# A hand-ordered attention and MoE kernel: both halves of V of pair 2 issued by ScalarE, of pair 3 by GpSimd, w_in issued further up, and the first quarter's loads and compute in another order

## The chip, the cores and the metric

The kernel runs on one core of one Trainium2 chip. The metric is the device time of one execution in microseconds (us). Before the change three runs took 309.12, 309.83 and 308.51 us, median 309.12. Five engines run their own instruction queues side by side: TensorE (PE), VectorE (DVE), ScalarE (ACT), GpSimd (POOL) and SyncE (SP), which here only issues transfers. ACT and POOL issue transfers too: those of SP and ACT go to hardware queues, those of POOL to a software queue. An engine works its queue strictly in order, so an instruction that waits holds up all that stand behind it on that engine.

## The reference

Attention over 8 batches, 8 heads, 576 tokens of 64 numbers, followed by a two-layer network over all 4608 tokens.

```python
q_d, k_d, v_d = means of q, k, v over groups of 4 tokens
out_d = softmax(scale * q_d @ k_d.T) @ v_d          # 144 x 144 per head
out_up = np.repeat(out_d, 4, axis=2)
mask = np.abs(pos[:, None] - pos[None, :]) < 4
scores = np.where(mask, scale * q @ k.T, -1e9)      # 576 x 576 per head, a band
attn_out = out_up + softmax(scores) @ v
x = attn_out as (4608, 512)
h = x @ w_in                                        # 512 x 2048
g = h - np.tanh(h)
result = g @ w_out                                  # 2048 x 512
```

## The kernel before

**Tiling.** Heads are worked in 32 pairs p (two heads side by side on the partitions), four pairs to a batch. Of the band only blocks around the diagonal are computed. Each batch of 576 tokens then goes through the network as one block: 512 of its tokens in 16 chunks of the hidden width, the remaining 64 of several batches together.

**What one pair does.** Its q and k (`st`, 256 KB each; for pairs 4 to 7 the buffers are named `Tw`) are cast to bf16 into `qr` (L550), transposed on PE (L557) and copied out of PSUM as `kt` (L562) and `kq` (L567). The last 64 tokens of all four pairs of a batch come as `sr`, are cast to `rr` (L540) and transposed and copied as `rT` (L580, L584), and each pair takes its part of them (L612, L617; "the rests"). Sums over four tokens are made on PE for the first pairs (L664, L667) and copied out as `qkd` (L672), and for later ones by adding on POOL or DVE through `half` (L649, L653, L643). Scores follow in two groups: the band (L701) and then the last band block with the pooled part (L711, L717); three exponentials on ACT write them to `E` (L722, L726, L730). The band part is multiplied by the mask (L757). V comes in two halves, one per head, as `vst` (160 KB each), is cast to `vw` (L476) and pooled by PE into `vp` (L507, L511). The product with V is L771; a reciprocal and a product on DVE (L787, L789) normalise it to `ln`, PE transposes that back (L814), and DVE joins the two parts into `xT` (L820, L807).

**The network.** For batch 0 the hidden layer takes a chunk of w_in and one column block of `xT` per matmul (L848), which lets it begin when the first pairs of the batch are ready; ACT takes the tanh (L860) and DVE subtracts (L863). w_in and w_out are loaded by POOL in four pieces each (L457, L461).

**What sets the order.** Every operation is recorded with what it reads and writes. `TURNS` is a table of numbers, two digits each, that lists all operations in the order in which they are emitted; it thereby sets the order on each engine. `ENGINES` gives, where an operation may run on more than one engine, a letter for the one that takes it (A, D or P). `BANKS` gives the PSUM bank of each tile, `FILL` puts dummy matmuls in front of some PE operations (17 ahead of the first, one at seven other places; L1524), and `BEHIND` adds waits that keep DVE and POOL in a chosen order at their common port to SBUF. Nothing is planned at run time. Transfers of the hardware queues take their completion semaphores in turn from a set of eight, counted over SP and ACT together: a new transfer waits until the eighth one before it has landed.

**The places that the change touches.** `load_v` (L407) issues the two halves of V of a pair; `ASIDE` (L301) lists the halves that ACT issues in place of SP: half 0 of pair 2 and half 0 of pair 3. Those two stand in ACT's queue behind the rests of pair 0 and 1 and ahead of `qkd` of pair 1. `load_w` issues the weights. The table's head up to about its 18th row, the first two rows of `ENGINES` and `BANKS`, and `FILL` and `BEHIND` hold what concerns the first batches.

Of the kernel before, what the change touches and what calls it, by code (L numbers as in the profile page):

```python
# [101 lines left out]
def kernel(  # L102
# [9 lines left out]
    nc = tc.nc  # L112
    B, H, S, D = q.shape
# [10 lines left out]
    STEP = 112  # L124
# [30 lines left out]
        "000I0J0G0H0307060E0F0K0L04050Q0R010O0P0W0X0e0f0C0M0N0S0T100Y0Z110g0h020a0b1215130D0A160U"  # L155
        "0V171H1P18141I0B1J191L1Q1A1K1R221M1N0m0n0i0j1O242R231T1j1k1B251S1C1f1d1g1e1u1U0c0d1W1v1w"
        "2S1y0k0l1x2Z091V2I2J0y2T082G2H1z1D2V291E2W0o0p261F2U1X1l1m212X27201n1o2z1Y2b1Z0z391p1q2a"
        "0q0r2d282c2n2o1r1G2e311h1i1s2f2p2q2g2A2K2L322Y1t3A3B2B2O2y5H2C3C3D302D2P3G5I332E1a353E0s"
        "0t2M2N5J34362v2h2F373N3O5K5L5P2i1b5e5f383F0u0v5M5S2w5N2r2s2j5O5Q3H5U5R3I3J5v662Q2k683K5B"
        "5T1c635E5V3L3d2l5C5x2m643j3k5y3M3l3e5D5F3f3g5X3p3q5W0w0x3m3h3v3r3n3w3i3P3Q5w3s5Y3t2t2u3o"  # L160
        "413x615k5l3y3u5z3z4243604744404D4E4548623T3U495Z654A464F4G4B4J6b5a674H4P3V3W4Q6B4R2x4K4L"
        "4I696c4S5g5h4M6e4C4N3X3Y3R3S5s5b6g6A4V4W4b4O6d4c5c4d4T4X5d4Y6U4h5t4U4i4Z5m5n4j4e4k6T4a6C"
        "4l4n6V6D4o6E4f4t4u4p6W4v4g6X6Z6f6F6Y7A6j4z4q6G5G4w4m504r513Z3a526H6a5556534s577B6Q4x5854"
        "7f7C6R7g4y6h3b3c7D597E72887F6i8d8e5A5u7I6k7G71896l7l6m74758E8F7H8j736n6y76778k6z966o7J6K"
        "6L977K6I6J9C7L5i5j7m8K6p5q5r7M6w6x8L7N7r7O5o5p8p78CF6M6N9D79CC7s6u6v7x9f8Q6q6r7y9g6s6t8R"
        "9Z9I9a8S8q9T9b9cCG7z9h9i7X9jCE6O6P7Y7b9k7P7Q7Z9J9l9v9w7c6SCB8v9t9u7d8w9U7V7WCD9O8x9P7R7S"
        "7eAA9m9W7h9V9X9Y7i7a7n9QCH7o7j9nAB7p7k7t70ACAD809d9o9p849eAGAd7uA1A27qAe9q9zA0AH7vA79r81"
        "7T7U9sA8BD857w82ELEMAIAh9x9y86838AAgAJ8B878GAiAjCI8H8C8MAEAM8VAFATAU8I8NAVAW8DAm8WAKAbAc"
        "Ao8J8O8ZB0B18XAL8aBGBH8fAq8PAn8gAN8Y8bBFB2B38l8h8cA9ApAk8m8iBEAt8rAOBMBIBJ8sAP8n8yAr8z8o"
        "8tDt92BcBdBN908u93AXAYBAAl91DyIgIh989EBaBbAs9FBBENEO94CJBOBPBgBh99BQ9K95Dx9AAuBiDzE09G9L"  # L170
        "9BBqEaBKBrBLE39HA5A6CLCMEJEKAv9MBsAwE4B8B9BtBRBkBlByBTEb9NE5A3A4BjE6E7BzEcEdBSCREACSCKAQ"
# [37 lines left out]
        "APADDADAADPPDDPPDDADDDDAPPDADDAADDDPDDDDDAADDADAADDDAAADDDPPAPPPAADAPPPDAAPAPADADPPPDDAA"  # L209
        "APADAAPPPDAAPPDDAAPPPDDAAAADDPDADDAADDDDAPPPDDPPDAAAPPAAPPDDAAPPPAAPPDDPPADDADDADAAPPDAP"  # L210
# [7 lines left out]
        "0123453012067016731120212706021330112130022310312010302101013121001113020110023303011200"  # L218
        "2131010210231012301102321001203101010110123031002311201210012130120131010102030210302321"
# [4 lines left out]
        "15717 2b71 2A71 3B41 2D11 5S31 3H31 6671"  # L224
    )
    BEHIND = (
        "0211 1H12 1D1V 0z20 1t2f 5I30 5Q5N 635B 5w5W 6562 6c2x 6d6A 5u6i AACD ABCH AmAF AnAL DxC"
        "J F8CZ FfFD DFFn MUFt GAGb IrJ6 JNK7 MZJs NBKu OELA LqNn ODLO O7OQ QoNy RYOp RZP8 T3Rd S"
        "WPQ PiSi TVTU TaRk TPUO TnUY TmTO WZU7 WeWc WfVu XWX6 XcXP Z5Yy ZqZ4 ZpZH"
# [71 lines left out]
    ASIDE = ((2, 0), (3, 0))  # L301
# [105 lines left out]
    def load_v(p):  # L407
        b, j, s = p // NP, p % NP, seat_v(p)
        for i in range(2):
            base = v[b, 2 * j + i]  # L410

            aside = (p, i) in ASIDE

            def issue(i=i, base=base, aside=aside):
                (nc.scalar if aside else nc.sync).dma_start(out=vst[s][:, i], in_=bass.AP(
                    tensor=base.tensor, offset=base.offset,
                    ap=[[D, 128], [STEP * D, NT], [1, D]]))
# [1138 lines left out]
```

## Time and profile before

| | |
|---|---|
| median of three runs | 309.12 us |
| profiled execution, its own time | 309.13 us |
| its span in the profile | 307.4 us |
| mean granted PE clock | 0.992 |
| PE busy | 296.4 us, 96% |
| DVE, ACT, POOL busy | 266.6, 224.1, 157.2 us |

The span runs from the first instruction to the last; 1.73 us of the profiled time lie around it. PE's time is given as busy time with the idle time ahead of an instruction put down to what ended it; a stretch of PE at the half clock counts as busy. In a line such as `L717 <- ACT qkd L672` the first line is what waited and the second what released it; tiles are shown without their buffer numbers, so `E` is that of either parity of pairs. A row of the timeline gives start and duration in us, and a row that ends in `q` after the engine's name (ACTq, SPq) is the issuing of a transfer.

### The profile page before, as it was taken

What the parts mean: (1) busy time and instruction counts of PE and PEld (TensorE: products, weight loads), DVE (VectorE), ACT (ScalarE), POOL (GpSimd) and SP (SyncE); (2) the same over time, 40 slices, a digit from 0 to 9 for tenths busy, and PEclk for the clock granted to TensorE, in tenths of its full rate; (3) what the DMA queues carried; (4) which work ended last, traced back from release to release, by engine and by line L of the source; (5) the groups of instructions that cost most, each with busy time, mean ns of one, the idle gap of its engine ahead of it and who ended that gap; (6) DMA issues with size and microseconds to landing.
All of it is one profiled execution on the core that took longest, in us unless ns stands there. A gap on an engine that the chain in (4) does not pass through costs nothing.

```text
span 307.4 us, 8109 instructions
## 1 busy us (share of the span) xinstructions
PE 296.4 (96%) x3091; PEld 210.9 (69%) x3100; DVE 266.6 (87%) x493; ACT 224.1 (73%) x403; POOL 157.2 (51%) x213
## 2 busy tenths in 40 slices
PE   8598999999999999999999999999999999999994
PEld 3476555545577755875577755555988888889983
DVE  2578888679998988999998889999999999998783
ACT  2588786279888786988958988898877898875300
POOL 5247756026864466337873278456524364626550
PEclk9979999999999999999999999999999999999999
DMA  7999999999999999999899999979989426000333
GB/s 220 271 264 249 246 228 152 210 235 220 218 241 281 242 216 234 291 175 273 210 262 220 284 222 173 278 193 260 188 227 218 146 28 189 1 3 2 136 122 87
DMA packets 121191, 60.83 MB, mean 198 GB/s; under 512 B 88896, under 2 KB 119104, under 8 KB 121152
## 3 DMA queue, kind: packets, MB, share of 16 engines
q1 hardware_dynamic: 114656, 54.94, 76.5%
q0 software_dynamic: 4224, 4.19, 8.3%
q10 hardware_dynamic: 2272, 1.18, 1.6%
q8 instruction: 24, 0.39, 0.5%
q14 instruction: 15, 0.12, 0.1%
HBM read 44.04 MB, written 9.44 MB: 174 GB/s over the span
## 4 chain that ended last, share of the span: by engine, by line
PE 88%; DVE 5%; DMA 4%; issue 1%; ACT 1%; ACTq 0%; SPq 0%; DVEq 0%
PE ps L1284 27%; PE ps L848 26%; PE ps L958 8%; PE ps L771 6%; PE ps L996 5%; PE ps L1142 4%; PE ps L701 3%; PE ps L1114 2%; PE ps L1081 2%; DMA st<-in_q_dram 2%; DMA sr<-in_q_dram 2%; PE ps L814 1%; DVE E L757 1%; PE ps L717 1%; PE ps L507 1%
## 5 line engine op out<-in xcount | busy, mean ns | idle before, releaser
L848 PE MATMUL ps<-xT,w_in_sb 128*128 128x512 bf16 x384 | 91.5, 379 | 0.0
L1284 PEld LDWEIGHTS <-gT 128*128 128x128 bf16 x672 | 64.5, 98 | 12.3
L863 DVE TENSOR_TENSOR gT<-ps,u 128x512 bf16<-128x512 f32 x96 | 64.2, 684 | 6.8 <-ACT u L860 5.6
L860 ACT ACTIVATE u<-ps 128x512 f32<-128x512 f32 x96 | 56.4, 599 | 16.3 <-PE ps L848 14.5
L848 PEld LDWEIGHTS <-w_in_sb 128*128 128x128 bf16 x384 | 35.4, 98 | 35.6
L550 POOL CAST qr<-st 128x512 bf16<-128x512 f32 x42 | 25.4, 613 | 41.3 <-DVE Tw L1193 15.5
L1284 PE MATMUL ps<-w_out_sb,gT 128*128 128x256 bf16 x336 | 43.4, 273 | 0.0
L1284 PE MATMUL ps<-Tw,gT 128*128 128x256 bf16 x336 | 42.5, 273 | 0.0
L722 ACT ACTIVATE E<-ps 128x912 bf16<-128x912 f32 x32 | 29.9, 934 | 7.1 <-PE ps L711 5.8
L789 DVE TENSOR_TENSOR ln<-ps,r 128x768 bf16<-128x768 f32 x32 | 30.6, 955 | 0.8
L628 ACT COPY kt<-kq 128x576 bf16<-128x576 bf16 x23 | 27.3, 1185 | 1.4 <-DMA kq<-qr 1.1
L757 DVE TENSOR_TENSOR E<-E,mask 128x1152 bf16<-128x1152 bf16 x31 | 23.5, 760 | 3.8 <-ACT E L726 3.5
L771 PEld LDWEIGHTS <-E 128*128 128x128 bf16 x576 | 21.9, 98 | 6.0 <-DVE E L757 1.4
L638 POOL TENSOR_TENSOR half<-kq 128x576 f32<-128x576 bf16 x16 | 20.5, 1279 | 8.4 <-ACT u L860 3.5
L730 ACT ACTIVATE E<-ps 128x576 bf16<-128x576 f32 x32 | 21.0, 657 | 1.4 <-PE ps L717 1.4
L771 PE MATMUL ps<-vw,E 128*128 128x65 bf16 x320 | 19.2, 195 | 1.3 <-DVE E L757 1.0
L643 POOL TENSOR_TENSOR qkd<-half 128x288 bf16<-128x288 f32 x21 | 16.7, 797 | 5.8 <-DVE r L787 2.0
L1219 DVE TENSOR_TENSOR gT<-gT 128x2048 bf16<-128x2048 bf16 x14 | 17.2, 1231 | 0.2
L1370 POOL TENSOR_TENSOR y<-y,keep 128x512 f32<-128x512 f32 x8 | 10.2, 1278 | 13.4 <-DVE E L757 4.8
L996 PE MATMUL ps<-xT,w_in_sb 128*128 128x128 bf16 x256 | 16.8, 219 | 0.0
L1306 ACT COPY y<-ps 128x512 f32<-128x512 f32 x19 | 11.0, 587 | 7.5 <-PE ps L1284 6.7
L771 PE MATMUL ps<-vpr,E 128*128 128x65 bf16 x128 | 16.5, 195 | 0.0
(183 smaller groups left out, 596.4 us busy)
## 6 DMA issues: line engine op xcount, KB each, us to landing
vst<-in_v_dram SPq DMA_DIRECT2D x54, 160.0 KB, 4.2
st<-in_q_dram SPq DMA_DIRECT2D x28, 256.0 KB, 3.7
st<-in_k_dram SPq DMA_DIRECT2D x28, 256.0 KB, 5.0
out_dram<-y SPq DMA_DIRECT2D x14, 512.0 KB, 4.3
v<-in_v_dram SPq DMA_DIRECT2D x20, 256.0 KB, 2.7
w_in_sb<-in_moe_w_in_dram POOLq DMA_DIRECT2D x4, 512.0 KB, 8.4
w_out_sb<-in_moe_w_out_dram POOLq DMA_DIRECT2D x4, 512.0 KB, 6.6
vr<-in_v_dram SPq DMA_DIRECT2D x8, 128.0 KB
```

What stands on the lines that cost most here:

```text
L550: (eng, ns, lambda dst=dst, src=src, fn=fn: fn(out=dst, in_=src), port)
L628: ("ACT", 1180, lambda: A.copy(out=ktv, in_=src), False),
L722: A.activation(out=E[s][:, :, E0:E0 + 456], in_=at(s1)[:, :, PS0:512], func=AF.Exp, scale=SCALE)
L757: eng.tensor_tensor(out=el, in0=el, in1=mask.unsqueeze(1).to_broadcast([128, 2, S]), op=ALU.mult)
L771: T.matmul(po[:, hh, 65 * n:65 * n + 65], E[s][:, hh, e:e + 128], vv, start=start, stop=stop)
L789: op("DVE", 960, lambda: V.tensor_tensor(out=ln[s].rearrange("p n (h d) -> p h n d", d=D), in0=blocks()[:, :, :, 0:64], in1=r[s].unsqueeze ...
L848: T.matmul(at(name)[:, 0, :], w_in_sb[:, dc, fc * 128:(fc + 1) * 128], xT[dc][:, c0:c0 + S].rearrange("p (c g) -> p c g", c=4)[:, :, 0:128 ...
L860: op("ACT", 600, lambda: A.activation(out=u[us], in_=at(name)[:, 0, :], func=AF.Tanh), reads=[("hd", kb, fc)], writes=[("u", us)], uses=[n ...
L863: op("DVE", 690, lambda: V.tensor_tensor(out=gT[g][:, fc, :], in0=at(name)[:, 0, :], in1=u[us], op=ALU.subtract), reads=[("hd", kb, fc), ( ...
L958: T.matmul(at(("hz", kb, G, bk))[:, 0, 256 * x:256 * x + 256], left(k, x), right(k), start=(first and x == 0 and k == 0), stop=(k == 1), s ...
L996: T.matmul(at(name)[:, 0, 128 * f:128 * f + 128], w_in_sb[:, dc, (f0 + f) * 128:(f0 + f) * 128 + 128], xT[dc].rearrange("p (b c g) -> p b ...
L1284: T.matmul(dst, left[:, f, 128 * j:128 * j + 128], right[:, f, :], start=(first and e == 0 and f == 0 and (j == 0 or apart)), stop=(e == 1 ...
```

## The change

`ASIDE` becomes a table `WAY` with the engine that issues each half of V: both halves of pair 2 go to ACT, both of pair 3 to POOL, all others stay on SP. The heads of `TURNS`, `ENGINES` and `BANKS` are others, and with them the order of the loads and of the compute of the first two batches. One line is added, so line numbers above 412 are higher by one.

```diff
-    ASIDE = ((2, 0), (3, 0))
+    WAY = {(2, 0): "ACT", (2, 1): "ACT", (3, 0): "POOL", (3, 1): "POOL"}
...
-            aside = (p, i) in ASIDE
-
-            def issue(i=i, base=base, aside=aside):
-                (nc.scalar if aside else nc.sync).dma_start(out=vst[s][:, i], in_=bass.AP(
-                    tensor=base.tensor, offset=base.offset,
-                    ap=[[D, 128], [STEP * D, NT], [1, D]]))
-            load(680 if aside else 500, issue, [("vst", s, i)], 940, 10 * p - 3000 + 5,
-                 eng="ACT" if aside else "SP")
+            eng = WAY.get((p, i), "SP")
+
+            def issue(i=i, base=base, eng=eng):
+                {"SP": nc.sync, "ACT": A, "POOL": GP}[eng].dma_start(
+                    out=vst[s][:, i], in_=bass.AP(
+                        tensor=base.tensor, offset=base.offset,
+                        ap=[[D, 128], [STEP * D, NT], [1, D]]))
+            load({"SP": 500, "ACT": 680, "POOL": 770}[eng], issue, [("vst", s, i)], 940,
+                 10 * p - 3000 + 5, eng=eng)
...
     FILL = (
-        "15717 2b71 2A71 3B41 2D11 5S31 3H31 6671"
+        "15717 2b71 2A71 3B41 2D11 5S31 3H01 6601"
     )
     BEHIND = (
-        "0211 1H12 1D1V 0z20 1t2f 5I30 5Q5N 635B 5w5W 6562 6c2x 6d6A 5u6i AACD ABCH AmAF AnAL DxC"
+        "0211 1H12 1u1A 2S1V 280y 2y3F 5C5W 5G6A 737H 9fCB 9UCE AhAg AnAF A9AL DyAs DxCJ F8CZ FfF"
```

Eighteen rows of `TURNS` and two each of `ENGINES` and `BANKS` differ. From the work on the left-over tokens of the first batches on, at about 84 us of the trace before, PE's order is the same in both; so is that of the other engines from about there on.

ACT's queue from its two transfers on, before (`vst2` and `vst3` are V of pairs 2 and 3, `E0` and `E1` the scores of even and odd pairs, `L726` the last band block, `L730` the pooled part):

```order
L415 DMA vst3_86<-in_v_dram 128x5x64
L415 DMA vst2_85<-in_v_dram 128x5x64
L672 CAST qkd1_100<-ps_138 128x2x144
L722 ACTIVATE E0_113<-ps_138 128x2x456
L726 ACTIVATE E0_113<-ps_138 128x2x120
L730 ACTIVATE E0_113<-ps_138 128x2x2x144
L562 COPY kt0_96<-ps_138 128x512
L476 CAST vw0_88<-vst0_83 128x10x64
L730 ACTIVATE E1_114<-ps_138 128x2x2x144
L722 ACTIVATE E1_114<-ps_138 128x2x456
```

And ACT's queue in the changed kernel, from a cast of q of pair 1 that POOL did before:

```order
L551 CAST qr1_93<-st1_74 128x2x4x64
L613 COPY kt0_96<-rT0_81 128x4x16
L415 DMA vst2_85<-in_v_dram 128x5x64 x2
L673 CAST qkd1_100<-ps_138 128x2x144
L723 ACTIVATE E0_113<-ps_138 128x2x456
L731 ACTIVATE E0_113<-ps_138 128x2x2x144
L727 ACTIVATE E0_113<-ps_138 128x2x120
L723 ACTIVATE E1_114<-ps_138 128x2x456
L551 CAST qr0_92<-st2_75 128x2x4x64
L731 ACTIVATE E1_114<-ps_138 128x2x2x144
L727 ACTIVATE E1_114<-ps_138 128x2x120
```

Both transfers are now V of pair 2, at the same place ahead of `qkd1`. Behind them ACT has the copy of `kt` and the cast of V of pair 0 no longer this early, and in their place, ahead of the odd pair's last exponentials, a cast to `qr0`: q of pair 2, which DVE did before as soon as it had landed.

POOL's queue behind the constants, before (`qr1` from `st1` is pair 1; `vrp` and `vpr0` are V sums of the last tokens):

```order
L550 CAST qr1_93<-st1_74 128x2x4x64 x2
L442 TENSOR_TENSOR vrp_107<-vrs_106 128x64
L550 CAST qr0_92<-st2_75 128x2x4x64
L445 TENSOR_TENSOR vpr0_111<-vrp_107,hsel_108 128x520
L476 CAST vw1_89<-vst1_84 128x10x64
L457 DMA w_in_sb_71<-in_moe_w_in_dram 128x4x512
L476 CAST vw3_91<-vst3_86 128x10x64
L550 CAST qr1_93<-Tw1_135 128x2x4x64 x2
L457 DMA w_in_sb_71<-in_moe_w_in_dram 128x4x512
L649 TENSOR_TENSOR half_98<-kt0_96 128x144x2
```

And in the changed kernel (`st3` is q of pair 3):

```order
L551 CAST qr1_93<-st1_74 128x2x4x64
L551 CAST qr0_92<-st2_75 128x2x4x64
L415 DMA vst3_86<-in_v_dram 128x5x64 x2
L551 CAST qr1_93<-st3_76 128x2x4x64
L458 DMA w_in_sb_71<-in_moe_w_in_dram 128x4x512
L758 TENSOR_TENSOR E1_114<-E1_114,mask_66 128x2x576
L477 CAST vw3_91<-vst3_86 128x10x64
L458 DMA w_in_sb_71<-in_moe_w_in_dram 128x4x512
L551 CAST qr0_92<-Tw0_134 128x2x4x64
L477 CAST vw2_90<-vst2_85 128x10x64
L541 CAST rr1_80<-sr1_78 128x2x4x64
L458 DMA w_in_sb_71<-in_moe_w_in_dram 128x4x512
```

The two halves of V of pair 3 are issued by POOL behind the cast of k of pair 2. The first piece of w_in stands directly behind the cast of q of pair 3, where it stood behind the cast of V of pair 1; the multiplication of `E1` by the mask, DVE's before, stands behind it on POOL, and the casts of V of pair 2 and of `rr1` are POOL's too.

On PE the sums of pair 1 (L664) stand ahead of the scores of pair 0, the pooled scores of pair 0 ahead of all scores of pair 1, and the transposes of q of pair 2 behind those of k of pair 3 and the pooled scores of pair 1. The sums of pairs 2 and 3 stand ahead of the pooling of V of pair 0 and the output of pair 0. Four groups that stood ahead of the first L848, namely the transposes of k and q of pair 5, the first scores of pairs 4 and 5, the back transposes of pairs 2 and 3, and the pooled scores and V pooling of pair 4, now stand between the first L848s or behind them. On SP the two second halves of V of pairs 2 and 3 are gone, the second half of pair 1 stands one place further up ahead of k of pair 4, V of pair 4 stands ahead of q and k of pair 5, and about five later loads stand ahead of the two first transposing transfers.

More of the change, by code (lines that the diff above doesn't have):

```diff
@@ L154 @@
     TURNS = (
[L155 to L169, printed above, removed]
@@ new lines @@
+        "1E1F0p5e0d0z2a1X2b2c2g1Y281Z2d1r1s1t1a1k0s1b1c1m302z1G2A2B3B3C2C2e2f3D2v2w2O2P3E3F2D3G2h"
+        "2i31353H322N362y0u2j333437380r3d2E2F5Q5I5P3I5R2k3j3k5S3e5U3J1q2l2m3K3L3p3q3v3w3M3f3g3r3s"
+        "2o3x3h2Q3t2H5H5T5X3i0t5E7T5F3l3m3y0w5V1i5B3u5J5L3n3z5K41422L5M5k4344404748492s3R5g4A3o4D"
+        "5O645N63655v3VAX4B4C4E4F3Q454J4K4L4G6s3T4M5w4666670v4P4V5W4Q4W4X4Y4N4H4I685h4O5C5D0x2u4Z"
+        "4a4R4S4T4U6B4b4c2x3X694d4h4i4j4e4f4g5x5y4n4o6q6U6t4k4l4p4q4r4t4u5z6T4m5Y5Z4z555f6050625m"
```

26 lines of the change are left out of this document (18 added, 8 removed).

## The prediction

> **What bounds the kernel now.** The page first:
>
> ```profile
> span 307.4 us, 8109 instructions
> PE 296.4 (96%) x3091; PEld 210.9 (69%) x3100; DVE 266.6 (87%) x493; ACT 224.1 (73%) x403; POOL 157.2 (51%) x213
> PE   8598999999999999999999999999999999999994
> ```
>
> PE is busy for 96% of the span, and the change takes no matmul away. What can be won or lost is PE's idle time, and the third row puts it at the start and in the last slice. The view by stretches of time says how much (columns: stretch; busy us of PE, its weight loads, DVE, ACT and POOL; granted PE clock; DMA share and rate):
>
> ```profile
> 10.00:15.00 5.00, 2.35 (x46) 1.83 (x41) 2.35 (x9) 1.85 (x4) 0.87 (x2) 1.00 1.18 266
> 15.00:20.00 5.00, 4.42 (x60) 3.71 (x59) 3.29 (x10) 4.21 (x10) 2.33 (x3) 0.66 1.20 272
> 20.00:25.00 5.00, 4.71 (x85) 3.66 (x84) 4.49 (x10) 4.80 (x11) 2.40 (x5) 1.00 1.16 234
> 25.00:30.00 5.00, 3.77 (x78) 2.92 (x77) 4.14 (x11) 4.40 (x10) 3.87 (x6) 1.00 1.20 264
> 30.00:35.00 5.00, 5.00 (x55) 2.97 (x54) 4.14 (x13) 3.49 (x8) 4.71 (x7) 1.00 1.21 213
> ```
>
> Idle time is 2.65, 0.58, 0.29 and 1.23 us in the first four rows, 4.75 together, and nothing from 30 us on. The orders of the two kernels meet again at about 84 us, so the tail is the same work. **The most that this change can win is therefore 4.75 us, and what the half clock of the second row costs; the most that it can lose has no such bound.** PE's waits from 7 to 31 us by cause (total, times, longest):
>
> ```profile
> PE ps L717 <- ACT qkd L672: 2.3, 1, 2.3
> PE ps L771 <- DVE E L757: 0.8, 1, 0.8
> PE ps L814 <- DVE ln L789: 0.4, 1, 0.4
> PE ps L771 <- DVE vp L511: 0.4, 1, 0.4
> PE ps L557 <- ACT E L722: 0.4, 1, 0.4
> PE ps L557 <- POOL qr L550: 0.3, 2, 0.2
> PE ps L664 <- ACT E L730: 0.2, 1, 0.2
> ```
>
> These sum to 4.8: the list is complete. The largest wait is followed back in the chain of waits (start, us, what) and in ACT's timeline:
>
> ```profile
> 6.86 5.86 DMA st<-in_q_dram
> 11.17 1.95 ACTq L415 DMA_DIRECT2D vst<-in_v_dram  x2
> 13.15 0.40 ACT L672 CAST qkd<-ps 128x288 bf16<-128x288 f32 x1 [3.82 <-DMA st<-in_q_dram]
> 13.45 0.94 ACT L722 ACTIVATE E<-ps 128x912 bf16<-128x912 f32 x1
> 14.27 0.38 ACT L726 ACTIVATE E<-ps 128x240 bf16<-128x240 f32 x1
> 14.52 0.67 ACT L730 ACTIVATE E<-ps 128x576 bf16<-128x576 f32 x1
> 15.05 0.62 ACT L562 COPY kt<-ps 128x512 bf16<-128x512 bf16 x1
> 17.95 0.68 ACT L550 CAST qr<-Tw 128x512 bf16<-128x512 f32 x1
> 25.89 0.31 ACT L617 COPY kq<-rT 128x64 bf16<-128x64 bf16 x1
> ```
>
> ACT has nothing to compute for 3.82 us, because its two V issues occupy its queue for 1.95 us, from 11.17 to 13.12. The second can't be issued before a load of q has landed at 12.72 (6.86 + 5.86), whose completion semaphore it takes over; only then comes qkd of pair 1, and PE, which needs it, stands still for 2.3 us.
>
> **The change part by part.**
>
> *The wait on qkd(1) stays: 0.* V of pair 2 stands in the same two places of ACT's queue as the two halves that it replaces, and the eight semaphores go round in the same order up to there, so its second half waits for the same load. What stands ahead on ACT, a 0.64 us cast of q of pair 1, fits into the 3.82 us. Bounds: −0.5, if that load lands earlier; +0.5, if the new traffic makes it later. I take 0: POOL's new transfers are issued behind a cast that now ends at about 12.2.
>
> *A new wait on the cast of q of pair 2: +1.4.* DVE makes it now, at 11.98, under cover of PE's long wait. In the changed kernel it is ACT's, behind qkd1 and four exponentials. From start to start ACT needs 0.82 for L722 (13.45 to 14.27), 0.25 for L726, 0.53 for L730. That gives 13.45 + 0.82 + 0.53 + 0.25 + 0.82 = 15.87 for the start and, with 0.64 to 0.68 us, 16.5 for its end. Two rows of the timeline before:
>
> ```profile
> 14.44 0.61 PE L557 MATMUL ps<-ident,qr 128*128 128x128 bf16 x8 [0.35 <-ACT E L722]
> 11.98 0.46 DVE L550 CAST qr<-st 128x512 bf16<-128x512 f32 x1 [0.78 <-DMA st<-in_q_dram]
> L550 POOL CAST qr<-Tw 128x512 bf16<-128x512 f32 x4 | 2.5, 614 | 0.8 <-PE ps L717 0.8
> L550 ACT CAST qr<-Tw 128x512 bf16<-128x512 f32 x3 | 1.9, 640 | 0.0
> ```
>
> The first shows the eight transposes of k and q of pair 2, begun when the first exponential gives a PSUM bank free; the second DVE's cast; the others are groups (count, busy us, mean ns). In the changed kernel PE has, until ACT's cast ends, only the pooled scores of pair 1 and the transposes of k of pairs 2 and 3, done by about 14.44 + 0.61 + 0.1 = 15.15. It then waits until 16.55. The cast of q of pair 3 isn't earlier: `BEHIND` puts it on POOL behind the first mask on DVE, which can start when L726 ends at about 15.2, takes 0.76, and the cast 0.61, so 16.6. Two legs end together, which makes the wait firm: 1.0 to 1.8.
>
> *What goes: −1.3.* Of the other six waits the mask (0.8) should go, since POOL takes the mask of pair 1 off DVE; the sums behind L730 (0.2) and the casts by POOL (0.3) now stand behind the long wait. The three of 0.4 (bank, `vp`, `ln`) stay: `vp` of pair 0 is made by ACT behind 14 other instructions, and `ln` has the same chain in front of it. Bounds −2.5 to −0.3.
>
> *Work that is only moved: 0.* The first L848 comes some 3 to 4 us earlier, at about 27; but the groups of pairs 2 to 5 that stood ahead of it now stand behind. PE is full from 30 us on, so it is the same work at another time. w_in earlier is needed for this and gains nothing by itself.
>
> *Waits behind the first L848: +0.3 and +0.5.* Before, the list of PE's waits from 31 to 85 us is empty. The scores of pair 4 need the rests of pair 4 from ACT. From qkd1 to that rest ACT has 28 rows in place of 25; 25 rows took 12.7 us (13.15 to 25.89, the last row of ACT's timeline above), 0.5 a row with waits, so it comes 1.5 later, while PE comes to the scores little later than before. L848s stand between them and cover most: 0.3 (0 to 1.0). Then POOL:
>
> ```profile
> L757 POOL TENSOR_TENSOR E<-E,mask 128x1152 bf16<-128x1152 bf16 x1 | 2.4, 2374 | 0.0
> L438 POOL TENSOR_TENSOR vrs<-vr 128x128 f32<-128x128 f32 x5 | 2.3, 457 | 2.4 <-DVE E L757 2.4
> L442 POOL TENSOR_TENSOR vrp<-vrs 128x64 bf16<-128x64 f32 x7 | 2.3, 322 | 4.4 <-DVE E L757 2.4 <-DVE vrs L438 1.9
> L757 DVE TENSOR_TENSOR E<-E,mask 128x1152 bf16<-128x1152 bf16 x31 | 23.5, 760 | 3.8 <-ACT E L726 3.5 <-ACT E L722 0.3
> L457 POOL DMA_DIRECT2D w_in_sb<-in_moe_w_in_dram x4 | 3.3, 820 | 0.0
> L643 POOL TENSOR_TENSOR qkd<-half 128x288 bf16<-128x288 f32 x21 | 16.7, 797 | 5.8 <-DVE r L787 2.0 <-DVE gT L1219 2.0 <-DVE E L757 0.8
> 15.59 1.06 POOL L445 TENSOR_TENSOR vpr<-vrp,hsel 128x520 bf16<-128x520 bf16 x1 [3.42 <-DVE vw L1453]
> POOL half L649 <- ACT kt L612: 3.3, 1, 3.3
> ```
>
> Up to the sums of pair 7 POOL gets the mask (2.4), two V issues (0.8 each by the row of w_in), the cast of `rr1` (0.6, as its casts of the same size above), a V sum (0.5) and one more issue of w_out (0.8), and loses `vpr` (1.06), one `vrp` (0.3) and one `qkd` (0.8): 5.9 less 2.2, +3.7 us. The last row, POOL's longest wait between 25 and 60 us, covers 3.3 of it. So the sums of pair 7 come at least 0.4 later, and its pooled scores with them, at about 50 us, where DVE and ACT have little slack: +0.5, from 0 (the L848s cover it) to 1.5 (half of the addition shows).
>
> *Sum:* 0 + 1.4 − 1.3 + 0 + 0.3 + 0.5 = **+0.9 us**. On the profiled execution's 309.13 (307.4 of span and 1.73 around it) this gives **310.0 us**; the median of the runs, 309.12, is the same to 0.01. A measurement of this kernel can tell about 0.5%, 1.55 us, from no change, so the forecast is no change, on the slower side.
>
> **The rivals.**
>
> *Slower: a second stretch at half clock, about 311.7.* Windows of 3.41 us, laid so that the half clock fills one:
>
> ```profile
> 8.93:12.35 3.42, 2.22 (x38) 1.56 (x38) 2.42 (x7) 0.41 (x2) 1.32 (x3) 1.00 1.19 278
> 12.35:15.76 3.41, 1.60 (x28) 1.39 (x29) 1.65 (x6) 2.61 (x6) 0.17 (x1) 1.00 1.20 254
> 15.76:19.17 3.41, 3.02 (x38) 2.59 (x35) 1.73 (x7) 3.17 (x7) 1.32 (x2) 0.50 1.19 270
> 19.17:22.58 3.41, 3.26 (x63) 2.52 (x63) 3.38 (x7) 2.65 (x7) 1.65 (x3) 1.00 1.14 262
> ```
>
> The clock was halved behind a window with 1.60 us of PE busy and not behind one with 2.22. In the changed kernel the window from 15.76 holds 0.8 us of the new wait and some 0.5 of that on `vp`, so about 2.1 busy where 3.02 were: just above. If the cast ends 0.5 us later it decides, and the next window's 3.26 us of work take up to 1.7 us more: 310.0 + 1.7. For it: both legs run close. Against it: at half clock the same matmuls fill the window longer. Chance 0.14. The Trainium skill, page "TensorE: Matmul & The Clock Gate", "Part 4: PE-mode transpose", says that transposes don't count as busy PE in the same way; the window in question would be rich in them. By that rule the second stretch would come, and the time be 311.7; the trace neither shows nor excludes it, since the window from 15.76 before held transposes beside the output of pair 0, and the clock came back.
>
> *Slower: the transfers get in each other's way, about 311.4.* The DMA share is 1.16 to 1.21 in every row from 10 to 35 us: nothing is free there. w_in moves ahead by 3 us or more (512 KB a piece) and V of pair 3 comes by a second queue, while V of pairs 0 and 1 and k of pair 4 are on their way. A transfer of 160 KB costs 160/265, 0.6 us, at the rate of these rows; both halves of pair 3 let into the middle put V of pair 0 back by up to 1.2 us, with its cast, its pooling and the first output behind it, and V of pairs 5 to 7 come later by as much as w_in took. 310.0 + 1.2, and some 0.2 by DVE at the port it shares with the POOL mask: 311.4. Against it: out(0) waits for ACT by then, not for V. It decides once V of pair 0 lands after 16 us. Chance 0.19. The Trainium skill, page "DMA: Bandwidth & Descriptors", section "Issuing engines are not separate DMA queues", says that other issuers save only the time of issuing; by it nothing is won by the new issuers, and the trace agrees, as ACT's 1.95 us of issuing is nearly all waiting for semaphores.
>
> *Faster: the stalls behind the first L848 don't come, about 307.5.* Then +0.3 and +0.5 fall away, and the early L848s fill the gaps at `ln` and `vp` too (−0.8, the rest of the bound of −2.5 but for one bank wait). And a wait that lies in the stretch at half clock costs no matmul at half speed: 0.8 us of it save up to 0.4. 309.13 + 1.4 − 1.3 − 0.8 − 0.4 = 308.0; with the new wait at its lower bound and the mask on both pairs out of the way another 0.5 less, 307.5. For it: PE without a single wait from 31 to 85 us before, so there is slack. Against it: ACT, busy 4.80 of 5 us from 20 to 25, gets more. Chance 0.27.
>
> **How the numbers follow.** Forecast (310.0, its own range 309.0 to 311.0) 0.40, second half clock 0.14, transfers 0.19, faster 0.27. Bounds for faster and slower are 307.57 and 310.67. Of the forecast 0.10 lies above the upper; of the clock 0.12 and the transfers 0.14; of the faster case 0.18 below the lower. Slower 0.36, faster 0.18, the same 0.46. The range leaves 0.1 below, within the faster case, and 0.1 above, in the two slower ones with their prices at the full: 307.4 to 312.2.
>
> **What would show it.** Right: PE's list still has about 2.3 behind qkd L673, a new row of 1.0 to 1.8 behind ACT's cast L551 (or POOL's), no 0.8 behind the mask; the first L849 at about 27; a wait of some tenths at the scores of pair 4 and one near 50 us at those of pair 7. Idle time up to 31 us would be near 5. Wrong: if the row behind qkd shrinks by a microsecond or more, the semaphores go round otherwise than I read them; if PE idles under 4 us to 31 and nothing after, the faster case holds; if the clock shows 0.5 for more than 3.41 us, the second.

## The result, and the profile after

The changed kernel took 313.54 us (median of four runs, 312.97 to 315.38), the kernel before 309.48 beside it; the ratio is 1.0154, 95% interval [1.0129, 1.0179]. It is slower, by 4.1 us, where 310.0 with no measurable change was forecast; the range ended at 312.2. The profiled execution is the longest of the four (315.38 of its own time, 313.7 of span), so a second profile of the same kernel was taken (312.7 of span); where the two differ, that is said.

The page of the changed kernel:

```profile
span 313.7 us, 8117 instructions
PE 297.8 (95%) x3090; PEld 211.9 (68%) x3100; DVE 267.7 (85%) x486; ACT 225.1 (72%) x407; POOL 161.9 (52%) x218
PE   7588999999999999999999999999999999999994
PEclk9959999999999999999999999999999999999999
```

PE's work is the same, its busy time 1.4 us longer and its idle time 4.9 us longer. The view by stretches (columns as in the prediction) puts some of it at the start:

```profile
10.00:15.00 5.00, 1.70 (x37) 1.39 (x35) 1.81 (x9) 0.97 (x2) 2.11 (x3) 1.00 1.13 251
15.00:20.00 5.00, 4.09 (x41) 3.40 (x41) 3.56 (x8) 4.69 (x12) 1.87 (x3) 0.54 1.21 258
20.00:25.00 5.00, 4.06 (x60) 3.32 (x60) 2.09 (x7) 3.35 (x7) 4.51 (x5) 0.78 1.17 279
25.00:30.00 5.00, 4.15 (x92) 3.48 (x92) 3.77 (x8) 3.04 (x8) 1.30 (x2) 1.00 1.18 254
```

Idle time is 3.30, 0.91, 0.94 and 0.85 us, 6.0 in place of 4.75, and the half clock holds for two windows of 3.41 us where it held for one. From 20 to 25 us DVE was busy for 4.49 us before and is for 2.09 now: it starves behind the late head. PE's waits from 7 to 31 us:

```profile
PE ps L702 <- ACT qkd L673: 3.2, 1, 3.2
PE ps L1525 <- DVE vp L512: 0.8, 1, 0.8
PE ps L581 <- ACT rr L541: 0.7, 1, 0.7
PE ps L558 <- ACT qr L551: 0.6, 1, 0.6
PE ps L558 <- ACT E L723: 0.4, 1, 0.4
PE ps L1525 <- ACT E L723: 0.4, 1, 0.4
PE ps L815 <- DVE ln L790: 0.3, 1, 0.3
PE ps L558 <- POOL qr L551: 0.2, 1, 0.2
```

The long wait on `qkd` is there as before and 0.9 longer (0.5 in the second profile); the row on `rr` is the first load being late in this execution. L1525 is the dummy matmul of `FILL`: a dummy, too, waits until its PSUM bank is free, here 1.2 us in all.

That isn't 4.1 us, and the rest is spread over the program. The table gives how much later PE starts the same instruction than in the profile before (median over the instructions of a stretch, us). Kernel names are those of the experiments; the first column is the start of the first transposes of the rests (7.18 us before), which shows how late the first loads were in that execution.

| kernel | first loads | 84 us | 96 us | 250 us | 265 us |
|---|---|---|---|---|---|
| before, again | +0.4 | 0.7 | 0.7 | 0.7 | 0.7 |
| after | +0.5 | 3.3 | 3.9 | 5.3 | 6.4 |
| after, again | +0.6 | 3.2 | 4.1 | 4.3 | 5.4 |
| h2: after to 29 us, then before | +0.2 | 3.0 | 3.0 | 3.3 | 3.3 |
| h4: after to 63 us, then before | −0.1 | 1.4 | 1.4 | 1.3 | 2.4 |
| h3: before to 63 us, then after | +0.1 | 0.4 | 1.2 | 2.0 | 3.1 |
| x3: after with nine dummies fewer | 0.0 | 1.0 | 1.5 | 1.8 | 1.8 |

A row is one execution. The traces of the kernels whose medians lie within 0.15% of the kernel before (e2, e4, x1, y1, y2) lag between −1.3 and +1.8 at 84 us, so the lag at 84 us is good to one or two microseconds only, and what is read from the table is the steps behind it.

The lag grows in steps and lies flat between them (0.2 us near 215 us aside). Three come back: one up to 84 us, one from 84 to 96, and one near 262 us, where both kernels run the same instructions. (A fourth, of 0.8 to 2.1 us near 165 us, is in the first profile of the changed kernel, in h1's and h3's, and in that of e4, which has the old order; it isn't in the second profile nor in h4 or x3, and so is taken as one of single executions.) What made them is the subject of the experiments.

### The profile page after: what moved, and what is told of

The parts are those of the page before. It is cut to its first block, busy times and chain, and to the rows that moved or that the text cites. A ratio compares the mean times of both kernels' runs of the same rounds, so it can differ in the third digit from the quotient of the medians.

```text
span 313.7 us, 8117 instructions
## 1 busy us (share of the span) xinstructions
PE 297.8 (95%) x3090; PEld 211.9 (68%) x3100; DVE 267.7 (85%) x486; ACT 225.1 (72%) x407; POOL 161.9 (52%) x218
## 4 chain that ended last, share of the span: by engine, by line
PE 46%; DVE 11%; DMA 5%; issue 4%; POOL 3%; SPq 2%; ACT 1%; POOLq 0%; DVEq 0%; ACTq 0%
PE ps L1285 17%; PE ps L849 16%; PE ps L959 3%; PE ps L997 3%; PE ps L772 2%; DMA v<-in_v_dram 2%; DVE gT L864 2%; DVE gT L1220 2%; DMA kq<-qr 2%; DMA lT<-ln 1%; PE ps L1082 1%; PE ps L702 1%; DVE S L1220 1%; DVE gL L1010 1%; DVE E L758 1%
## 5 line engine op out<-in xcount | busy, mean ns | idle before, releaser
L849 PE MATMUL ps<-xT,w_in_sb 128*128 128x512 bf16 x384 | 92.1, 380 | 1.0 <-ACT y L1307 1.0
L849 PEld LDWEIGHTS <-w_in_sb 128*128 128x128 bf16 x384 | 35.3, 98 | 36.3 <-issue 1.4
L723 ACT ACTIVATE E<-ps 128x912 bf16<-128x912 f32 x32 | 29.8, 933 | 6.7 <-PE ps L712 5.6
L644 POOL TENSOR_TENSOR qkd<-half 128x288 bf16<-128x288 f32 x21 | 17.4, 831 | 4.6 <-DVE gT L1220 2.0
```

Of the source, the lines that this page charges most:

```text
L723: A.activation(out=E[s][:, :, E0:E0 + 456], in_=at(s1)[:, :, PS0:512], func=AF.Exp, scale=SCALE)
L849: T.matmul(at(name)[:, 0, :], w_in_sb[:, dc, fc * 128:(fc + 1) * 128], xT[dc][:, c0:c0 + S].rearrange("p (c g) -> p c g", c=4)[:, :, 0:128 ...
```

## The experiments

Sixteen other kernels ran, each beside runs of the kernel before on the same chip (its medians there: 308.9 to 309.6 us), and the two kernels themselves once more for their profiles.

**Issuers apart from order.** e1 gives the changed kernel the old issuers; e2 gives the kernel before the new ones, POOL's two behind its cast of k of pair 2.

```diff
e1, on the changed kernel (the four loads in TURNS moved to match):
-    WAY = {(2, 0): "ACT", (2, 1): "ACT", (3, 0): "POOL", (3, 1): "POOL"}
+    WAY = {(2, 0): "ACT", (3, 0): "ACT"}
e2, on the kernel before (the four loads in TURNS moved to match):
-    ASIDE = ((2, 0), (3, 0))
+    WAY = {(2, 0): "ACT", (2, 1): "ACT", (3, 0): "POOL", (3, 1): "POOL"}
```

> The changed kernel's order of compute with the issuers of before: ACT issues half 0 of V of pairs 3 and 2, SP the other two halves, POOL none. Theory A (the new issuers cost: V of pair 3 by the software queue runs into the first loads, holds q of pair 3 and so qkd of pair 1 back, and keeps POOL busy) expects 310 to 311 us and PE's wait behind qkd near 2.3 us. Theory B (the new order of compute costs, above all the late cast of q of pair 2 and the second window at half clock) expects 312.5 to 314 us with two windows of 3.4 us at half clock, as in the changed kernel.

> The kernel before with the new issuers alone: both halves of V of pair 2 on ACT at the place of the old two, both of pair 3 on POOL behind the cast of k of pair 2, all else in the old order. Theory A (issuers) expects 311.5 to 313.5 us, theory B (order) 309 to 310 us with one window at half clock.

e1: 318.40 us, ratio 1.0297 [1.0279, 1.0314], outside what either theory expected. e2: 309.19, ratio 1.0010 [0.9991, 1.0030]. The issuers alone cost nothing in the old order, and in the new order they save 4.9 us: without them PE waits 2.7 us at the pooling of V (L508) for POOL's casts. The loss is the order's.

**The half clock.** Ten dummies in front of the first scores of pair 1 (e3), nine at the same wait before (e4).

```diff
e3, on the changed kernel:
-        "15717 2b71 2A71 3B41 2D11 5S31 3H01 6601"
+        "15717 2b71 2A71 3B41 2D11 5S31 3H01 6601 24710"
e4, on the kernel before:
-        "15717 2b71 2A71 3B41 2D11 5S31 3H31 6671"
+        "15717 2b71 2A71 3B41 2D11 5S31 3H31 6671 2539"
```

> The changed kernel with ten dummy matmuls ahead of the first scores of pair 1, where PE stands still for qkd. Theory C (the clock: PE's long wait empties one window and the work behind it doesn't fill the next, so two windows of 3.4 us run at half clock) expects both gone, or at least the second, and 311 to 312.3 us; at most 2 x 1.7 us can be had. If the waits, not the clock, set the time of that stretch, the time stays above 313 although the clock is full.

> The kernel before with nine dummy matmuls at the same kind of place, ahead of the pooled scores of pair 1. Theory C expects the one window at half clock gone and 307.8 to 308.8 us; if PE waits for other engines in that stretch anyway, 309 to 309.6.

e3: 312.99, ratio 1.0118 [1.0088, 1.0147]. e4: 309.39, ratio 1.0014 [0.9995, 1.0033]. The clock is full in both. The view by stretches of e3 shows why no more came of it:

```profile
15.00:20.00 5.00, 3.82 (x71) 3.25 (x72) 3.58 (x10) 4.34 (x12) 3.44 (x3) 1.00 1.17 252
20.00:25.00 5.00, 3.49 (x59) 2.48 (x58) 3.96 (x10) 4.05 (x8) 2.94 (x5) 1.00 1.18 280
```

At full clock PE is busy for 7.31 of these 10 us in place of 8.15 and waits the more: the matmuls at half speed stood beside waits on ACT. Two windows at half clock cost 0.55 us together by the medians, 1.1 by the ratios, whose intervals overlap. What the one window costs in the kernel before stays open: e4's trace runs 1.2 us ahead of it at 84 us and gives 1.0 back near 262 us, at the step that is explained below and that the kernel before doesn't have.

**Late casts, and the mask on POOL.** e5 gives the casts of q of pairs 2 and 3 back to DVE, early; e6 gives DVE the mask of pair 1. In both the moved operations also stand further up in `TURNS`, and one pair of `BEHIND` is gone.

```diff
ENGINES, first row, on the changed kernel
-        "DAADDADADDDDAPPADDDDDDDDPPAADAAAPDAPDPDADADDDDDPPAAAAAADDPPPDPPADAAAPPPDAAAAAAAAAPPPDADA"
e5
+        "DAADDADADDDDAPPADDDDDDDDPPDADAAAPDAPDDDADADDDDDPPAAAAAADDPPPDPPADAAAPPPDAAAAAAAAAPPPDADA"
e6
+        "DAADDADADDDDAPPADDDDDDDDPPAADAAADDAPDPDADADDDDDPPAAAAAADDPPPDPPADAAAPPPDAAAAAAAAAPPPDADA"
```

> The changed kernel with the casts of q of pairs 2 and 3 back on DVE, early in its queue, as before. Theory D (the late casts are the first loss, and what follows hangs on them) expects 311 to 312.3 us and no wait of PE behind a cast. Theory E (the loss is spread over the first 30 us, DVE standing idle while ACT and POOL do its work, and over the waits behind them) expects 312.7 to 313.5.

> The changed kernel with the mask of pair 1 back on DVE (0.76 us) in place of POOL (2.37 us). Theory F (the slow mask on POOL holds up the second output, POOL's casts of V and the chain behind them) expects 311.5 to 312.7 us; theory E expects 313 to 313.6, as DVE has room there and the output of pair 1 waits for other things.

e5: 312.81, ratio 1.0105 [1.0076, 1.0133]; e6: 313.34, ratio 1.0121 [1.0093, 1.0148]. The late casts are worth 0.7 us by the medians (1.5 by the ratios), which is the order of the wait of 0.6 to 0.9 in the list; the mask on POOL costs nothing that shows. Both times are what theory E expected.

**Where in the order.** The tables of the two kernels were joined at one operation: all that stands ahead of it in one kernel's `TURNS`, with its engines, banks, dummies and port waits, then the rest in the other's sequence. h1 and h2 join at 29 us, h3 and h4 at the first scores of pair 8 (63 us). Two more profiles of the two kernels themselves show what repeats.

> A mixed order: the order and issuers of before up to the last back transpose of pair 3, about 29 us, and behind that the remaining operations in the sequence of the changed kernel. Theory E (the loss arises before the first network matmul) expects 309 to 310.5 us. Theory G (it arises behind it, in the sequence from 30 to 84 us) expects 311.5 to 313.5.

> The other mix: order and issuers of the changed kernel up to its first network matmul, and behind that the remaining operations in the sequence of before. Theory E expects 312 to 314 us, theory G 309 to 310.5.

> The kernel before, unchanged, profiled once more. If the steps that the changed kernel's trace shows behind 84 us (some 0.5 us at 85 to 95, 1.1 at 165, 1.1 at 255 us) belong to its order, this trace has none of them, as the first one had none; if they come and go with the timing of transfers, some may stand here too.

> The changed kernel, unchanged, profiled once more: about 313.3 us. The two windows at half clock and the steps at 85 to 95 and 255 us should be there again; the one at 165 us, and the first loads' delay of half a microsecond, need not, since the first profiled execution was 1.8 us longer than the three others.

> The order before up to the first scores of pair 8 (63.5 us in the trace before), the changed kernel's order behind them. Theory P, the part from 29 to 63 us makes the second loss (there the pooled scores of pairs 5 to 7 wait for their sums): nothing of it is left, 309.0 to 310.0, and the first L996 within 0.5 us of before's 83.7. Theory Q, the part from 63 to 84 us makes it by what it leaves to DVE: 311.5 to 313.5, as with the cut at 29 us, with first L996 to the end at 225.5 or more in place of 223.7.

> The mirror image: the changed kernel's order up to the first scores of pair 8, the order before behind them. P: head and middle are both there, 312.5 to 314.0, no less than the cut at 29 us gave (312.89). Q: only the head's loss is left, 311.0 to 312.9, with first L996 to the end at 223.7 to 224.2.

h1: 313.44, ratio 1.0122 [1.0085, 1.0159]. h2: 312.89, 1.0117 [1.0082, 1.0152]. h3: 311.50, 1.0093 [1.0063, 1.0123]. h4: 312.25, 1.0108 [1.0072, 1.0145]. The second profiles: 309.83 before, 314.44 after. Neither theory alone holds: each part of the new order loses on its own, and the parts don't add, since a later head gives the engines behind it time to catch up. What repeats is a rule over all kernels: the step from 84 to 96 us is there where the stretch from 63 to 84 us has the new sequence (after twice, e1, e3, e5, e6, h1, h3, x2, x3; y3, below, stalls ahead of it and lacks it) and absent where it has the old (before twice, e2, e4, h2, h4, x1, y1, y2). DVE's timeline in h3 shows what differs:

```profile
84.87 0.96 DVE L757 TENSOR_TENSOR E<-E,mask 128x1152 bf16<-128x1152 bf16 x1
86.47 1.67 DVE L1219 TENSOR_TENSOR S<-gT 128x2048 bf16<-128x2048 bf16 x1
92.95 0.75 DVE L757 TENSOR_TENSOR E<-E,mask 128x1152 bf16<-128x1152 bf16 x1
93.62 0.94 DVE L1193 TENSOR_TENSOR Tw<-w_out_sb,Tw 128x1024 bf16<-128x1024 bf16 x1
94.49 1.21 DVE L1219 TENSOR_TENSOR gT<-gT 128x2048 bf16<-128x2048 bf16 x1
```

The same place in DVE's timeline of h4, which has the old sequence there:

```profile
86.51 0.75 DVE L758 TENSOR_TENSOR E<-E,mask 128x1152 bf16<-128x1152 bf16 x1
87.18 1.22 DVE L1220 TENSOR_TENSOR S<-gT 128x2048 bf16<-128x2048 bf16 x1
93.53 0.75 DVE L758 TENSOR_TENSOR E<-E,mask 128x1152 bf16<-128x1152 bf16 x1
94.20 1.22 DVE L1220 TENSOR_TENSOR gT<-gT 128x2048 bf16<-128x2048 bf16 x1
```

Between the mask and the sum `gT` h3 has the last of eight sums of w_out, L1193, and PE waits for `gT`; PE's waits in h3 have the row, and h4's have none there:

```profile
PE ps L1284 <- DVE gT L1219: 0.5, 1, 0.5
```

Before, that sum ran at 75.58 us, in a stretch (68 to 84 us) in which DVE was idle for 1.4 us; the changed kernel runs it at 96.6, in one (84 to 100 us) with 0.25 us. Its row in DVE's timeline before:

```profile
75.58 0.68 DVE L1193 TENSOR_TENSOR Tw<-w_out_sb,Tw 128x1024 bf16<-128x1024 bf16 x1
```

The view by stretches before, around the place where it now stands (9.41 us of DVE in 10):

```profile
82.00:92.00 10.00, 9.95 (x133) 7.38 (x134) 9.41 (x12) 8.70 (x16) 7.54 (x11) 1.00 1.25 218
```

Its row in DVE's timeline of the changed kernel:

```profile
96.61 0.68 DVE L1194 TENSOR_TENSOR Tw<-w_out_sb,Tw 128x1024 bf16<-128x1024 bf16 x1
```

The view by stretches of the changed kernel, where DVE has 9.90 us in 10 ahead of it:

```profile
85.00:95.00 10.00, 9.90 (x142) 7.54 (x138) 9.90 (x14) 8.95 (x17) 7.95 (x10) 1.00 0.97 212
```

h3's first mask and `S` are longer besides (0.96 and 1.67 for 0.75 and 1.22): POOL works through `half`, `qkd` and a cast beside them. That the sequence from 63 to 84 us makes the step is shown by h3 and h4; that it does so through this one sum is read from the rows, since no run moved the sum alone. The same is seen in the group of four of the eight sums (count, busy us, mean ns), before:

```profile
L1193 DVE TENSOR_TENSOR Tw<-w_out_sb 128x1024 bf16<-128x1024 bf16 x4 | 2.7, 684 | 0.0
```

The same group of the changed kernel:

```profile
L1194 DVE TENSOR_TENSOR Tw<-w_out_sb 128x1024 bf16<-128x1024 bf16 x4 | 3.6, 940 | 0.0
```

The one of the four that makes the difference, in DVE's timeline of the changed kernel:

```profile
65.15 1.71 DVE L1194 TENSOR_TENSOR Tw<-w_out_sb 128x1024 bf16<-128x1024 bf16 x1
```

And POOL's timeline at the same moment:

```profile
65.03 1.28 POOL L639 TENSOR_TENSOR half<-kq 128x576 f32<-128x576 bf16 x1 [4.48 <-PE ps L1143]
```

The sum that takes 0.68 alone took 1.71 when it began 0.12 us behind a POOL addition of 1.28. The Trainium skill, page "SBUF — State Buffer", section "Who interferes with whom", says that of two such operations of DVE and GpSimd the one that comes second waits for the whole of the first; the last two rows agree to 0.13 us (0.68 and what is left of 1.28 make 1.84, against 1.71).

**V all on SP, or V of pair 2.** To take ACT out of the issuing and the long wait on `qkd` with it:

```diff
x1, on the kernel before:
-    ASIDE = ((2, 0), (3, 0))
+    ASIDE = ()
x2, on the changed kernel:
-    WAY = {(2, 0): "ACT", (2, 1): "ACT", (3, 0): "POOL", (3, 1): "POOL"}
+    WAY = {(3, 0): "POOL", (3, 1): "POOL"}
```

> The kernel before with all halves of V issued by SP, at the same places of the common sequence. ACT then has nothing that waits for a semaphore ahead of qkd of pair 1. Expected: PE's 2.3 us wait behind qkd shrinks to under 0.5. If what is won before 31 us reaches the end, 307.3 to 308.3 us; if it is given back to other waits, 308.8 to 309.6.

> The changed kernel with V of pair 2 issued by SP instead of ACT, pair 3 still by POOL. Expected: PE's 3 us wait behind qkd gone, the exponentials and the cast of q of pair 2 about 2 us earlier. If the head decides, 311 to 312 us; if the sequence from 30 to 84 us and what hangs on it decides, above 312.5.

x1: 309.00, ratio 1.0007 [0.9988, 1.0026]; x2: 312.36, 1.0134 [1.0075, 1.0193]. The cast `qkd` of pair 1 moves from 13.15 to 10.88 us in x1, the largest wait is gone and so is the half clock, and nothing is won. PE's waits in x1 from 7 to 31 us, the first two:

```profile
PE ps L507 <- POOL vw L476: 1.7, 1, 1.7
PE ps L814 <- DVE ln L789: 1.0, 2, 0.6
```

And the first three in x2:

```profile
PE ps L508 <- ACT E L727: 2.0, 1, 2.0
PE ps L558 <- ACT qr L551: 1.1, 1, 1.1
PE ps L508 <- ACT vw L477: 0.9, 1, 0.9
```

In x1 the wait moves to the casts of V: POOL's first, for which PE waits the 1.7 us, begins at 18.83 behind DVE's mask, and two later ones wait 1.8 and 2.2 us for V itself, which lands later. In x2 PE waits at the same line for the last exponential and then for V's cast. A stall taken out at one place comes back at the next; that the loads set the pace of the whole head is a reading that no run isolates.

**The step near 262 us.** There DVE waits for a transposing transfer in the changed kernel and not before. Its row in DVE's timeline:

```profile
264.62 0.53 DVE L808 TENSOR_TENSOR xT<-lT 128x336 bf16<-128x336 bf16 x2 [1.12 <-DMA lT<-ln]
```

PE's timeline right behind it:

```profile
265.20 0.93 PE L959 MATMUL ps<-xT,w_in_sb 128*128 128x256 bf16 x7 [0.69 <-DVE xT L808]
```

A transfer counts as landed when each of 16 shares has reported. In the trace's transfer records 15 shares of this one report at 262.85 to 262.98 and one at 264.6. The second profile, h1 and x2 show the same, one share 1.6 to 1.7 us behind. In the other seven kernels with the step (e1, e3, e4, e5, e6, h3, h4) all 16 report together and late: 3.6 to 3.9 us behind the transposing transfer ahead of this one, where they come 2.1 us behind it in all kernels without the step. At the same time PE's own code is fetched: the queue view of the changed kernel from 262.5 to 263.2 us has one such packet beside the transfer's. (That the code is PE's is inferred: the queue has 24 packets of 16 KB in an execution, one to about 258 of PE's 6204 recorded instructions.)

```profile
DMA packets 68, 0.28 MB, mean 399 GB/s; under 512 B 3, under 2 KB 3, under 8 KB 67
q1 hardware_dynamic: 67, 0.26, 96.0%
q8 instruction: 1, 0.02, 8.6%
```

In every kernel with the step (the changed one twice, e1, e3, e4, e5, e6, h1, h3, h4, x2) this fetch stands 905 to 928 recorded PE instructions ahead of the program's end, where all kernels run the same instructions, and begins 0.3 to 1.7 us ahead of the time at which the transfer would land by the usual 2.1 us; in those without it (before twice, e2, x1, h2) it stands 870 ahead of the end and begins 1.6 us behind the landing. e4 is the old order with nine dummies more, and has the step. x3 moves the fetch and changes nothing else of the order: it has nine dummies fewer ahead of it. y3 takes out seven of the nine, and y1 and y2 the same seven from kernels without the step.

```diff
x3 and y3, on the changed kernel:
-        "15717 2b71 2A71 3B41 2D11 5S31 3H01 6601"
+        "15715"
+        "15717"
y1, on the kernel before, and y2, on x1:
-        "15717 2b71 2A71 3B41 2D11 5S31 3H31 6671"
+        "15717"
```

> The changed kernel with nine dummy matmuls taken out of FILL (15 warm-up ones in place of 17, none of the seven single ones), so that PE's instruction fetch near 262 us comes 18 instructions later in PE's program. Theory H, that fetch delays one of the sixteen shares of the transposing transfer at that time: DVE's wait of 1.1 us on DMA ahead of L808 there and PE's wait of 0.5 to 0.8 behind it go, first L996 to the end falls from 225.8 by about 1.1, and the time is 312.0 to 312.6. Theory I, the delay belongs to the order of the first 84 us (what DMA engines still have queued): the wait stays and the time is 313.0 to 313.6.

> The changed kernel without the seven single dummies, the 17 warm-up ones kept: the fetch comes 14 instructions later in PE's program, against 18 in the run with nine taken out. Theory H (fetch meets transfer): the wait of 1.1 us on the transposing transfer is gone again, first L996 to the end is 224.4 or less, the time 310.8 to 311.8. Theory I: the wait is there, 312.2 or more.

> The kernel before without the seven single dummy matmuls in FILL (the 17 warm-up ones stay). Theory R, the dummies stand in PE's full stretch of 19 to 40 us and cost their own time there, 0.21 us apiece (512 columns; six or seven of them): 1.3 to 1.7 us less, 307.6 to 308.1, unless a window of half clock comes back. Theory S, they fill time in which PE waits anyway: 309.0 to 309.6. The instruction fetch moves later, away from the transposing transfer, so no step at 255 us either way.

> All V issued by SP (the run that gave 309.0) and the seven single dummies taken out as well. R: 307.3 to 307.9; S: 308.7 to 309.4.

x3: 311.15 (310.62 to 313.87, seven runs, two of them above 313), ratio 1.0084 [1.0047, 1.0120], 2.4 us below the changed kernel. y3: 312.22, 1.0099 [1.0069, 1.0129]. y1: 309.23, 1.0008 [0.9989, 1.0026]; y2: 309.40, 1.0001 [0.9981, 1.0022]. In x3, y3, y1 and y2 the fetch stands 870 instructions ahead of the end, as in the kernel before, and 1.6 us behind the landing; x3 and y3 thus moved it by about 36 instructions of the fixed part and not by the 18 and 14 that were taken out. DVE has no wait there. Its timeline in x3:

```profile
259.96 0.52 DVE L808 TENSOR_TENSOR xT<-lT 128x336 bf16<-128x336 bf16 x2
260.26 0.52 DVE L808 TENSOR_TENSOR xT<-lT 128x336 bf16<-128x336 bf16 x2
```

So the step of 1.1 us goes when the fetch goes. y3 missed its numbers (225.4 us from the first L996 on for 224.4, and a time that theory I expected, although the wait is gone), and shows the same thing at another place: an earlier fetch now meets a load. Waits of POOL in y3 from 80 to 90 us:

```profile
POOL qr L551 <- DMA st<-in_q_dram: 1.8, 1, 1.8
```

Fifteen shares of that load of q report at 83.19 to 83.44 us and one at 85.12; the fetch begins at 83.05. PE's lag rises there from 1.8 to 3.4.

The same is found all over the twenty traces, the kernel before included. Behind 20 us they have 145 transfers whose last share reports over 1.2 us behind the other fifteen. At 110 of them such a fetch begins between 1.5 us ahead of the first share's report and 0.5 us behind it, which holds for only 334 of all 3031 transfers counted. In the kernel before, too, the fetch at 259.2 us goes with a late share, of the next transfer (1.8 us, at 260.3), and PE has no wait behind it. The step near 262 us is thus a matter of which transfer the fetch meets.

The dummies' own price: in the kernel before nothing (y1, y2), so they fill time in which PE waits. In the changed kernel x3 lags 1.0 at 84 us where the second profile lags 3.2, of which 0.6 is its late first load: 1.6 us less, and the rows of 0.8 and 0.4 on L1525 are gone from its list. (In both executions a share of nearly every early load reports about 1.0 us late, so that doesn't tell them apart; see below.)

## Why the prediction was wrong, point by point

**Failed: "the tail is the same work".** The prediction took from this that nothing can be lost behind 84 us, and set moved work at 0. From the first L996 on (the first matmul of the left-over tokens, 83.7 us before) the tail took 225.9 us (second profile) or 226.6, against 223.7 before. Two things were missed. The orders do not meet on DVE at 84 us: one sum of w_out stands there 21 us later in the program, on a DVE with no room, and the prediction had only PE's order in view for that statement. The sequence that puts it there makes 0.5 to 1.0 us from 84 to 96 us in the kernels that have it and no other stall ahead of it; that this sum does it, with POOL's additions beside DVE's, is read from the rows. And the same instructions took 1.1 us longer near 262 us, because other code ahead moved a fetch of PE's code onto a transfer that DVE waits for. No row that the prediction shows pointed to this, and no range was allowed for it.

**Mis-sized: the head and the first L848s, +0.9 forecast, +2.6 measured at 84 us** (3.2 in the second profile less 0.6 for its first load). The two profiled executions are the longest of the kernel's five; by the medians, 4.1 less the 2.2 of the steps behind it, the head's part is an estimated 1.9. By terms:

- The wait on `qkd` stays: right. It grew by 0.5 (second profile) to 0.9; the bound was +0.5. POOL's V stood at 10.18 us, not behind 12.2, but the growth is another thing: the load of q that ACT's second issue waits for landed at 13.28 (second profile) with 15 of its shares in by 12.21; before, it landed at 12.72 with 14 in by 12.17. One share of nearly every load from 11 to 18 us reports 0.9 to 1.4 us behind the rest in both profiles, with no fetch of PE's code before 18.5. That doesn't follow the order: it is about 0.1 or less in e3 and h4, which have the new order's head, and up to 1.7 in e2 and y1, which have the old one's.
- The new wait on the cast of q of pair 2: there, 0.6 to 0.9 for 1.4; e5 gives it 0.7. ACT began the cast at 16.73 for the 15.87 worked out, so the mechanism holds and PE had more to do meanwhile than was counted.
- What goes, −1.3: the mask (0.8) and L730 (0.2) went. The wait at `vp`, expected to stay at 0.4, became 0.8 and came on a dummy, and a bank wait of 0.4 came on another. The waits of dummies had no term in the sum; with nine dummies out, 1.6 us go.
- Waits behind the first L848: none at the scores of pair 4 (0.3 forecast); 0.6 at the pooled scores of pair 7 (0.5 forecast), through the sums as described; the last of them was DVE's, which itself waited 0.5 for POOL's `half`:

```profile
55.20 0.30 PE L718 MATMUL ps<-qkd 64*128 64x144 bf16 x4 [0.55 <-DVE qkd L644]
```

- The first L849 was expected at about 27 us and came at 30.4 (29.8 in the second profile), against 30.9 before: the head's lag ate what the order moved up. That h2, with the old order behind 29 us, lags 3.0 at 84 us and h4 only 1.4 suggests that the new order wins some 1.6 back from 29 to 63 us, as it was meant to (by the medians, h4's 1.0 near 262 us taken off, 3.3 and 1.9); from 63 us on it loses again.

**The rivals.** The second half-clock window came, with a chance of 0.14: the windows from 15.36 on hold 2.81 and 3.33 us of busy PE at half clock.

```profile
15.36:18.77 3.41, 2.81 (x27) 2.13 (x27) 2.62 (x6) 3.10 (x7) 1.31 (x2) 0.51 1.17 264
18.77:22.18 3.41, 3.33 (x45) 3.22 (x43) 0.98 (x3) 2.75 (x8) 2.73 (x2) 0.50 1.27 227
22.18:25.60 3.42, 2.56 (x49) 1.86 (x47) 2.15 (x6) 2.25 (x4) 2.33 (x4) 0.99 1.13 326
```

Its place was right, its price of 1.7 us was not: e3 takes both windows away for 0.55 (1.1 by the ratios). By the rule that the prediction quotes from the Trainium skill, page "TensorE: Matmul & The Clock Gate", section "Part 4: PE-mode transpose", the clock would stay down; it did, but whether by transposes or by the gaps no run here separates. The transfers did not decide: the two halves of V of pair 0 landed at 11.8 and 14.3 us, 0.7 and 0.8 later than before with first loads 0.5 late, and not after 16; e2 puts the new issuers alone at nothing. ACT's 1.95 us of issuing, which that rival called nearly all waiting, are 0.79 of issuing and 1.16 of waiting in the trace before; and that other issuers win nothing holds in the old order (e2) and not in the new, where e1 lost 4.9 us without them. The faster case failed with the forecast.

**The sum of what was found**, for the second profile: 0.6 by the first load, 2.6 to 84 us, 0.9 to 96, 0.2 between, 1.1 near 262, 5.4 together. The medians of the runs differ by 4.1, as that execution ran 0.9 above its kernel's median. Left open: how the head's 2.6 divides beyond the casts (0.7), the clock (0.55 to 1.1) and the dummies (up to 1.6), which overlap, and the late shares of that execution; whether the one sum of w_out makes the whole step behind 84 us; and in which way a fetch holds up a share, since only its place was varied. No version beat the kernel before: e2, e4, x1, y1 and y2 all lie within 0.15% of it.

## What to carry to other kernels

Before setting moved work at nothing, compare the order of every engine to the place where the last one meets again, and ask of each moved operation whether its engine has room at the new place; here the sequence that moves a DVE operation from a stretch with slack to a full one cost about as much as the largest new wait at the start. A stall at the start is worth what is left of it at the next wait, not its length: taking 2.3 us of wait away gave nothing. Where a program's tail slows by about a microsecond without a change in its instructions, look for a late transfer and a code fetch at the same time, and move the code by some dummies to see whether it goes. One trace's lag at the start says little: executions of kernels of equal time differ there by 3 us.

## What was not expected of the hardware

A fetch of PE's code (one packet on the queue marked "instruction", 0.9 to 1.5 us long at the transposing transfer) while a transfer runs goes with that transfer landing 1.5 to 1.8 us late. Where the fetch begins 0.3 to 0.4 us ahead of the usual landing, one of the 16 shares is late (the changed kernel twice, h1, x2), as at the load of q in y3; where it begins 0.4 to 1.7 us ahead, all 16 are (seven kernels). The delay is gone from the transposing transfer when the fetch is moved by about 36 instructions, as x3 and y3 do by leaving out nine and seven dummies. The Trainium skill, page "DMA: Bandwidth & Descriptors", section "Why a DMA increments its semaphore by 16 and not by 1", says that the engines of a transfer finish independently and only the full count means that all data landed; the records of the changed kernel agree, 15 shares within 0.13 us and the wait until the last.

Two windows at half clock with PE busy for 2.81 and 3.33 of 3.41 us cost 0.55 us by the medians of e3 and the changed kernel (1.1 by their ratios), well under the 1.7 us that half speed for one window alone could take: at full clock PE waits 0.84 us more in the 10 us around them.
